# A pause on GpSimd and two later negations on ScalarE, ahead of the first out-projection of a fused attention and feed-forward kernel

## The chip, the cores and the metric

The kernel runs on one core of a Trainium2 chip. Time is device time in microseconds of one execution. The kernel before took 953.59 us, the median of three runs (953.5 to 954.16). The engines are named as in the profile: PE is TensorE (PEld its weight loads), DVE is VectorE, ACT is ScalarE, POOL is GpSimd, SP is SyncE, which here only issues transfers.

## The reference

Two blocks follow each other. The first is attention over 4 batches, 8 heads, 768 positions and 64 channels, in which a query sees only the keys that chose the same one of 16 centroids. The second is a feed-forward block over the resulting 3072 x 512 matrix.

```python
mask = q_assign[:, :, :, None] == k_assign[:, :, None, :]
scores = np.where(mask, scale * np.matmul(q, k.transpose(0, 1, 3, 2)), -1000000000.0)
attn = softmax(scores) ; x = (attn @ v) as (3072, 512)
h = x @ w_in                      # w_in 512 x 2048
sp = np.maximum(h, 0.0) + np.log1p(np.exp(-np.abs(h)))
g = h * erf(sp)                   # the gate
out = g @ w_out                   # w_out 2048 x 512
```

All of it is in float32.

## The kernel before

The attention ends about 404 us into the span. What follows is the feed-forward block, in six chunks of 512 tokens, n = 0 to 5. This case is about chunk 0 alone, from 404 to 500 us, and there about three stages: `hidden(0, 0)` and `hidden(0, 1)`, the in-projection of two lots of columns of `w_in`, and `project26(0)`, the out-projection.

**In-projection.** Each `hidden` runs four blocks (j = 0 to 3). A block is a product of 2 x 2 parts by seven matmul groups (Winograd's form of Strassen's scheme): `ORDER = (1, 2, 6, 7, 5, 3, 4)`. Each group of 4 matmuls writes one of eight PSUM banks, in turn ("bank" or "turned" in the profile), and DVE adds that bank into the result tiles `g` (the rows `g<-bank,g` and `g<-turned,g`), so that a bank is free again eight groups later. The first evacuation of a block is a plain copy, by ACT in `hidden(0, 0)` and by DVE in `hidden(0, 1)`.

**The side work.** After each of the 28 groups of a `hidden` one piece of the list `aside_work` is emitted, in order. These 28 places are called slots here, 0 to 27. Every engine runs its instructions in the order in which they are emitted. The gate of chunk 0 is made by quarters: first quarter (lot 0, blocks 0 and 1), second (lot 0, blocks 2 and 3), third (lot 1, blocks 0 and 1), fourth (lot 1, blocks 2 and 3). For each, ACT runs a Softplus and an Erf curve over two 128x1024 halves into `a_s` (for the fourth quarter into `x_own`), and DVE then makes four products `g<-a_s,g` of 128x512.

**The weight forms.** The out-projection multiplies `g` by sums and differences of quarter blocks of `w_out`, called forms. POOL makes them, two 128x512 operations a form:

- `early_forms26`, `next_forms26` (from 413 us) and then `all_sums`, four integer additions on `w_out`, which end at 430.85 us;
- `middle_forms26`: `of_last_rows` (5 operations: the rest of the forms y0 and y1, `ring[2]`, the rest of slot 0) and `of_all_rows` (4 operations: slot 7 and `ring[1]`);
- `late_forms26`: `streamed` (2 operations into `ring[2]`), `turned_over` (ACT: slot 4 becomes the negative of `ring[1]`, slot 5 that of a block of `w_out`) and `kept` (4 operations, slots 3 and 6, and then two accumulating transfers on POOL's queue: slot 4 += y0, slot 5 += y1; the rows `DMA_DIRECT2D more_out<-x_own`).

y0 and y1 lie in the second `x_own` tile; slots 0, 3 to 6 in `more_out`, `w_out` blocks and the like; the `ring` tiles are `g_more` in the profile.

**Out-projection.** `project26(0)` takes 26 steps, p = 0 to 25, of 8 matmuls each; the right factor of step p is `RIGHT[p]`: a slot, a block of `w_out`, or, from 100 up, a form held in a tile that is filled again during the stage by `rest_of_forms26`. That function also emits, behind certain steps:

- p = 2: SP fills y0 with a block of `w_out` (`x_own<-w_out`); ACT writes the negative of slot 0 into y1;
- p = 3: POOL issues y0 += slot 6 and y1 += slot 1 (`x_own<-more_out`); SP stores both to memory (`b_dram<-x_own`);
- p = 5: SP fills `ring[2]` (`g_more<-b_dram`); p = 7: SP fills `ring[1]` (`g_more<-w_out`), ACT writes the negative of slot 1 into the first `x_own`, and POOL issues `ring[1]` += that (`g_more<-x_own`).

Step p = 7 multiplies slot 4, p = 9 y0, p = 13 y1, p = 16 `ring[1]` as just filled, p = 19 slot 5. The left factors are `g` blocks, or sums of them that DVE makes (`left_step`; the first three of them run in slots 21 to 23 of `hidden(0, 1)`).

SP issues in this order: the five stores of forms, the fill of y0, the store of y0, the fills of `ring[2]` and `ring[1]`, the store of y1, and so on. The list below shows the functions at their lines; nearly all instructions bear line 123, that of the class `InOrder`, so they are told apart by tile and time.

Of the kernel before, what the change touches and what calls it, by code (L numbers as in the profile page):

```python
# [14 lines left out]
ALU = mybir.AluOpType  # L15
# [32 lines left out]
N_LATE = 4  # L48
# [83 lines left out]
def kernel(  # L132
# [13 lines left out]
    te, ve, ae, ge = (  # L146
        InOrder(tc, e, in_order) for e in (nc.tensor, nc.vector, nc.scalar, nc.gpsimd)
    )

    def pool(name, bufs, **kw):  # L150
        return ctx.enter_context(tc.tile_pool(name=name, bufs=bufs, **kw))
# [106 lines left out]
    for base, pattern, sign, op, fill in (  # L258
# [5 lines left out]
            out=first, in_=first, compare_op=op, fill=fill, base=base, pattern=pattern,  # L264
# [376 lines left out]
    def lefts(a11, a12, a21, a22, new):  # L641
        return {1: a11, 2: a12, 3: new[2], 4: a22, 5: new[0], 6: new[1], 7: a21}

    def rights(b11, b12, b21, b22, new):
        return {1: b11, 2: b21, 3: b22, 4: new[2], 5: new[0], 6: new[1], 7: b12}
# [4 lines left out]
    def w_in_parts(f, n):  # L650
        c1, c2 = slice(f * P, (f + n) * P), slice((HF + f) * P, (HF + f + n) * P)
        return (
            w_in[:, 0:HK, c1], w_in[:, HK:, c1], w_in[:, 0:HK, c2], w_in[:, HK:, c2],
            [more_in[:, i, :, c1] for i in range(3)],
        )

    def x_parts(n):
        x = x_of[n]
        return (
            x[:, 0:HK, 0:HT], x[:, 0:HK, HT:], x[:, HK:, 0:HT], x[:, HK:, HT:],  # L660
            [x_more[:, i] for i in range(3)],
        )

    g_of = {}

    ORDER = (1, 2, 6, 7, 5, 3, 4)
    aside_work = []
# [13 lines left out]
    def fresh(c11, c12, c21, c22, first=ae.copy):  # L681
        return {
            1: [lambda m: first(out=c12, in_=m)],
            2: [lambda m: plus_of(c11, m, c12)],
            6: [lambda m: onto(c12, m)],
            7: [lambda m: plus_of(c21, m, c12)],
            5: [lambda m: onto(c12, m), lambda m: plus_of(c22, m, c21)],
            3: [lambda m: onto(c12, m)],
            4: [lambda m: minus_of(c21, c21, m)],
        }  # L690

    def block(pieces, after, done=lambda i: None, pace=1):

        for i in ORDER:
            m = bank()
            pairs_of = pieces(i)
            for k, (lhsT, rhs) in enumerate(pairs_of):
                te.matmul(m, lhsT=lhsT, rhs=rhs, start=(k == 0), stop=(k == len(pairs_of) - 1))
            for f in after[i]:
                f(m)  # L700
            done(i)
            for work in aside_work[:pace]:
                work()
            del aside_work[:pace]

    def finish_aside():
        for work in aside_work:
            work()
        aside_work.clear()

    def hidden(n, lot, between={}, pace=1, **kw):

        for s in range(2):
            g_of[n, s, lot] = gp.tile([P, 2, FG, HT], F32, name="g")
        x = rights(*x_parts(n))
        for j in range(FG):
            w = lefts(*w_in_parts(lot * FG + j, 1))
            a, b = (g_of[n, s, lot] for s in range(2))
            block(
                lambda i: [(w[i][:, k], x[i][:, k]) for k in range(HK)],  # L720
                fresh(a[:, 0, j], b[:, 0, j], a[:, 1, j], b[:, 1, j], **kw), pace=pace,
            )
            between.get(j, lambda: None)()
# [4 lines left out]
    def idle(n):  # L728
        return [lambda: None] * n
# [12 lines left out]
    def slot(i):  # L742
        if i in BLOCK_OF:
            return w_block(BLOCK_OF[i])
        return more_out[:, HOME[i] // 2, (HOME[i] % 2) * FG : (HOME[i] % 2 + 1) * FG]
# [17 lines left out]
    def store_form(k, t):  # L763
        nc.sync.dma_start(out=stored_form(k), in_=t)

    def formed(o, a, b, sign, f):
        (plus_of if sign > 0 else minus_of)(o[:, f : f + 2], a[:, f : f + 2], b[:, f : f + 2], ge)

    def formed_whole(o, a, b, sign):
        for f in (0, 2):  # L770
            formed(o, a, b, sign, f)

    def onto_by_dma(o, a):
        ge.dma_start(out=o, in_=a, accum_op=ALU.add)

    def negated(o, a):
        ae.activation(out=o, in_=a, func=ACT.Copy, scale=-1.0)
# [4 lines left out]
    def form_places(n):  # L782
        t = x_of[n].rearrange("p k t -> p (k t)")
        return [t[:, i * FG * HM : (i + 1) * FG * HM].rearrange("p (f m) -> p f m", f=FG) for i in range(2)]
# [6 lines left out]
    def next_forms26():  # L791
        w, y = w_block, form_places(1)
        store_form(3, ring[0])
        formed_whole(slot(2), w(5), slot(1), 1)
        formed(y[0], w(3), w(7), -1, 0)
        formed(y[1], w(6), w(7), -1, 0)
        formed(slot(0), w(1), w(7), 1, 0)

    def middle_forms26():
        w, y = w_block, form_places(1)  # L800

        def of_last_rows():
            formed(y[0], w(3), w(7), -1, 2)
            store_form(7, y[0])
            formed(y[1], w(6), w(7), -1, 2)
            store_form(8, y[1])
            formed_whole(ring[2], w(6), y[0], 1)
            store_form(6, ring[2])
            formed(slot(0), w(1), w(7), 1, 2)

        def of_all_rows():
            formed_whole(slot(7), w(2), ring[2], -1)
            formed_whole(ring[1], w(0), w(4), 1)
            store_form(1, ring[1])

        return [of_last_rows, of_all_rows]

    def late_forms26():
        w, y = w_block, form_places(1)

        def streamed():
            formed_whole(ring[2], w(3), slot(2), -1)
            store_form(0, ring[2])

        def kept():
            formed_whole(slot(3), w(5), y[0], -1)
            formed_whole(slot(6), w(5), ring[1], -1)
            onto_by_dma(slot(4), y[0])
            onto_by_dma(slot(5), y[1])

        def turned_over():
            negated(slot(4), ring[1])
            negated(slot(5), w(1))

        return [streamed, turned_over, kept]
# [72 lines left out]
    def split_gate(lot, half):  # L908
        products_of = []

        def curves():
            soft, erf, products = gate26(0, lot, half)
            run(f() for f in soft + erf)
            products_of.extend(products)

        return curves, [lambda i=i: products_of[i]() for i in range(4)]

    def gate_work(n, lot, half, also=(), wait=0):
        soft, erf, products_of = gate26(n, lot, half)
        return [lambda: run([f() for f in soft + erf]), *idle(wait), *also, *idle(8 - len(also) - wait), *products_of]  # L920
# [392 lines left out]
    def run(work):  # L1313
        for _ in work:
            pass
# [136 lines left out]
    for e in range(2):  # L1452
        ve.tensor_copy(
            out=ccT[e * D : (e + 1) * D, :, e * C : (e + 1) * C],
# [8 lines left out]
    for r in (0, D):  # L1463
        for half in range(2):
            for e in range(2):
                c = r + half * Q + e * C
                ve.tensor_copy(
                    out=pick[r : r + D, half, e * D : (e + 1) * D].rearrange("p (n c) -> p n c", n=2)[:, :, 1 : C + 1],
# [44 lines left out]
    last = divide(u - 1)  # L1513
# [9 lines left out]
    behind = pool("behind", 1).tile([P, 1], F32, name="behind")  # L1523

    def finish_attention():
        run(last)
        banks[:] = [None] * 6 + turned
# [12 lines left out]
    def weights(n):  # L1540
        return [functools.partial(w, N_EARLY + n) for w in (size_and_rest, bounded, sign, shifted)]

    def all_sums():
# [4 lines left out]
    first_half, first_products = split_gate(0, 0)  # L1548
    second_half, second_products = split_gate(0, 1)
    aside_work += (  # L1550
        idle(3) + sum((weights(n) for n in range(N_LATE)), []) + [first_half, all_sums, *middle_forms26(), *idle(3), *first_products]
    )
    hidden(0, 0, {0: lambda: (finish_attention(), next_forms26())})

    def last_half():
        finish_aside()
        first_steps = [functools.partial(left_step, 0, x) for x, step in enumerate(LEFT_STEPS) if step[0] < 0]
        aside_work.extend(gate_work(0, 1, 0, first_steps, 6))

    aside_work += [second_half, *late_forms26(), *idle(4), *second_products]  # L1560
    hidden(0, 1, {1: last_half}, first=ve.tensor_copy)
    finish_aside()
    project26(0)
# [43 lines left out]
```

## Time and profile before

| | before |
|---|---|
| median of three runs | 953.59 us |
| the profiled execution | 953.27 us |
| its span | 951.6 us |
| PE busy | 942.7 us (99%) |
| DVE busy | 789.8 us (83%) |
| ACT busy | 556.4 us (58%) |
| POOL busy | 504.3 us (53%) |

The span runs from the first to the last instruction that the profile shows; the profiled execution's own time is 1.67 us longer. In a timeline each row gives the start and the duration in microseconds, the engine, the line, the operation, output and inputs, their shape, and how many equal instructions in a row were merged ("x2"); brackets behind it give the idle time of the engine before it and what ended that. "SPq" is a transfer as SP issues it; the duration is that of the issue, not of the transfer.

### The profile page before, as it was taken

Reading aid. Unit: us, or ns where it says so; the run is one execution under the profiler, and the core shown is the slowest. Engines: PE = TensorE matmul, PEld = TensorE weight load, DVE = VectorE, ACT = ScalarE, POOL = GpSimd, SP = SyncE. Lnnn points to the kernel's source line nnn. Section 1 sums busy time; section 2 is a strip of 40 time slices with the busy share of each in tenths; the row PEclk is TensorE's granted clock in tenths of the full one; section 3 lists DMA queues with packets and bytes.
Section 4 is the critical chain, followed back from the end, with each engine's and each line's share of the span. In section 5 each row is a group of like instructions: output and inputs, shape, how many; then the busy total and the mean of one; then the engine's idle time right before and its main releaser. Section 6 shows DMA issues by size and latency. Waiting matters only on the chain.

```text
span 951.6 us, 22455 instructions
## 1 busy us (share of the span) xinstructions
PE 942.7 (99%) x8938; PEld 719.8 (76%) x8938; DVE 789.8 (83%) x1402; ACT 556.4 (58%) x854; POOL 504.3 (53%) x355
## 2 busy tenths in 40 slices
PE   8999999999999999999999999999999999999998
PEld 3555555555555555588888888998999899989987
DVE  8888888888888887888886688688868977897887
ACT  3777777887777777566513642654257236525541
POOL 1688888888888888899109211360064016103600
PEclk9999999999999999999999999999999999999999
DMA  9355555555454522032786247353444436343533
GB/s 214 73 113 113 113 112 104 120 112 104 103 117 84 132 59 58 18 120 111 199 250 237 101 103 201 127 191 111 155 146 154 133 111 211 111 155 123 155 112 111
DMA packets 175385, 123.14 MB, mean 129 GB/s; under 512 B 131632, under 2 KB 142384, under 8 KB 175280
## 3 DMA queue, kind: packets, MB, share of 16 engines
q1 hardware_dynamic: 170912, 116.29, 43.4%
q0 software_dynamic: 1872, 4.98, 2.9%
q8 instruction: 71, 1.16, 0.5%
q10 hardware_dynamic: 2496, 0.43, 0.2%
q14 instruction: 34, 0.28, 0.1%
HBM read 91.78 MB, written 23.33 MB: 121 GB/s over the span
## 4 chain that ended last, share of the span: by engine, by line
PE 93%; DVE 2%; ACT 1%; issue 1%; DMA 1%; POOL 1%; SPq 0%; DVEq 0%; ACTq 0%; POOLq 0%
PE bank L123 40%; PE turned L123 31%; PE sc L123 17%; PE wide L123 6%; DVE g L123 1%; POOL more_out L123 1%; ACT a_s L123 0%; DMA g_more<-in_moe_w_out_dram 0%; DVE nmx L123 0%; DMA in_k<-in_k_dram 0%; ACT L123 0%; SPq L123 0%; DVE kT L123 0%; ACT osb L123 0%; ACT w_out L123 0%
## 5 line engine op out<-in xcount | busy, mean ns | idle before, releaser
L123 POOL TENSOR_TENSOR more_out<-more_out,pr 128x768 f32<-128x768 f32 x128 | 217.2, 1697 | 15.9 <-ACT pr L123 6.5
L123 DVE TENSOR_REDUCE nmx<-wide 128x2 f32<-128x1024 f32 (+2 forms) x189 | 179.4, 949 | 40.3 <-PE wide L123 39.3
L123 ACT ACTIVATE pr<-sc 128x768 f32<-128x768 f32 x192 | 148.7, 810 | 79.9 <-PE wide L123 66.0
L123 PE MATMUL turned<-pr,in_v 128*32 128x193 f32 x3072 | 144.8, 330 | 0.0
L123 POOL TENSOR_TENSOR g<-g 128x512 f32<-128x512 f32 x36 | 47.2, 1311 | 180.7 <-DVE g L123 178.8
L123 PEld LDWEIGHTS turned<-pr,in_v 128*32 128x32 f32 x3072 | 91.5, 109 | 51.0 <-issue 21.9
L123 DVE TENSOR_TENSOR g<-g 128x512 f32<-128x512 f32 x132 | 90.7, 687 | 22.5 <-PE bank L123 11.4
L123 PE MATMUL sc<-qT,kT 64*128 64x384 f32 x528 | 98.3, 485 | 0.0
L123 DVE TENSOR_TENSOR g<-bank,g 128x256 f32<-128x256 f32 (+1 forms) x128 | 64.6, 530 | 16.1 <-PE bank L123 9.5
L123 PE MATMUL bank<-g_more,g 128*128 128x256 f32 x320 | 75.6, 379 | 0.0
L123 PE MATMUL bank<-x_own,w_in 128*128 128x128 f32 (+1 forms) x440 | 74.0, 310 | 0.0
L123 ACT ACTIVATE a_s<-g 128x1024 f32<-128x1024 f32 x38 | 39.5, 1054 | 56.9 <-POOL g L123 45.3
L123 POOL TENSOR_TENSOR more_out<-pr,pr 128x768 f32<-128x768 f32 x32 | 58.9, 1842 | 20.2 <-ACT pr L123 20.2
L123 DVE TENSOR_TENSOR g<-a_s,g 128x512 f32<-128x512 f32 x76 | 67.3, 904 | 0.4 <-ACT a_s L123 0.4
L123 PEld LDWEIGHTS bank<-g_more,g 128*128 128x128 f32 x320 | 60.8, 190 | 8.3
L123 PEld LDWEIGHTS bank<-x_own,w_in 128*128 128x128 f32 x440 | 63.1, 191 | 4.6 <-issue 0.6
L123 PE MATMUL wide<-kv,qv 64*128 64x512 bf16 (+2 forms) x378 | 64.9, 327 | 1.0 <-ACT km L123 0.6
L123 PE MATMUL bank<-w_out,g 128*128 128x256 f32 x280 | 64.5, 379 | 0.0
L123 PE MATMUL wide<-km,qm 32*128 32x512 bf16 (+2 forms) x378 | 62.4, 326 | 0.0
L123 ACT ACT_TABLE_LOAD x40 | 51.3, 1283 | 18.3 <-DVE g L123 17.7
L123 PEld LDWEIGHTS sc<-qT,kT 64*128 64x128 f32 x528 | 47.8, 187 | 18.6 <-issue 0.9
L123 PEld LDWEIGHTS <-qv 64*128 64x128 bf16 x384 | 24.6, 93 | 47.1 <-issue 29.6
(239 smaller groups left out, 2030.4 us busy)
## 6 DMA issues: line engine op xcount, KB each, us to landing
g_more<-b_dram SPq DMA_DIRECT2D x52, 512.0 KB, 3.3
g_more<-w_dram SPq DMA_DIRECT2D x84, 256.0 KB, 2.9
x_own<-in_moe_w_in_dram SPq DMA_DIRECT2D x13, 512.0 KB, 5.4
in_v<-in_v_dram SPq DMA_DIRECT2D x32, 192.0 KB, 3.2
x_dram<-more_out SPq DMA_DIRECT2D x128, 48.0 KB, 1.7
x_own<-x_dram SPq DMA_DIRECT2D x6, 1024.0 KB, 5.8
in_k<-in_k_dram SPq DMA_DIRECT2D x59, 96.0 KB, 2.8
in_q<-in_q_dram SPq DMA_DIRECT2D x58, 96.0 KB, 5.0
```

What stands on the lines that cost most here:

```text
L123: ins = getattr(self.engine, name)(*args, **kw)
```

## The change

Four things change, all in the side work of chunk 0.

- POOL's `middle_forms26` leave slots 21 and 22 of `hidden(0, 0)`. They now stand in slots 6 and 7 of `hidden(0, 1)`, behind a new POOL instruction, `hold`, which adds one element per partition of the last product of the first quarter to itself, into the one-column tile `behind`, and so waits for that product.
- The four products of the first quarter, of which DVE had two in slots 26 and 27 of `hidden(0, 0)` and two in slots 0 and 1 of `hidden(0, 1)`, all stand in slots 0 to 3 of `hidden(0, 1)`.
- The second quarter's curves move from slot 2 to slot 4; `streamed` moves from slot 3 to slot 8; the second quarter's products stay in slots 10 to 13.
- `turned_over` and `kept` move from slots 4 and 5 to slots 15 and 16, behind the third quarter's curves in slot 14. ACT's two negations thus follow the third quarter's curves instead of preceding them.

The order of the instructions on PE and SP is the same as before. On POOL only `hold` is new.

```diff
@@ -1548,16 +1548,24 @@
     aside_work += (
-        idle(3) + sum((weights(n) for n in range(N_LATE)), []) + [first_half, all_sums, *middle_forms26(), *idle(3), *first_products]
+        idle(3) + sum((weights(n) for n in range(N_LATE)), []) + [first_half, all_sums, *idle(7)]
     )
     hidden(0, 0, {0: lambda: (finish_attention(), next_forms26())})
+
+    streamed, turned_over, kept = late_forms26()
 
     def last_half():
         finish_aside()
         first_steps = [functools.partial(left_step, 0, x) for x, step in enumerate(LEFT_STEPS) if step[0] < 0]
-        aside_work.extend(gate_work(0, 1, 0, first_steps, 6))
-
-    aside_work += [second_half, *late_forms26(), *idle(4), *second_products]
+        work = gate_work(0, 1, 0, first_steps, 6)
+        work[1:3] = turned_over, kept
+        aside_work.extend(work)
+
+    def hold():
+        last = g_of[0, 1, 0][:, 1, 0, 0:1]
+        ge.tensor_tensor(out=behind, in0=last, in1=last, op=ALU.add)
+
+    aside_work += [*first_products, second_half, hold, *middle_forms26(), streamed, *idle(1), *second_products]
     hidden(0, 1, {1: last_half}, first=ve.tensor_copy)
     finish_aside()
     project26(0)
```

## The prediction

> **What bounds the kernel now.** I read the page's span and chain first, then PE's waits over the whole span, then the timelines of PE, DVE, POOL, ACT and SP between 400 and 500 us, then SP's waits there. The first line is of the page, the second of its chain, the third of PE's waits.
>
> ```profile
> span 951.6 us, 22455 instructions
> PE 93%; DVE 2%; ACT 1%; issue 1%; DMA 1%; POOL 1%; SPq 0%; DVEq 0%; ACTq 0%; POOLq 0%
> PE turned L123 <- DVE g L123: 0.9, 2, 0.5
> ```
>
> PE carries the end. Whatever stops PE between here and the end is added to the time, and nothing behind gives it back. In the stages of the change PE waits only twice, 0.9 us together, both for DVE. That is all that the change can win there. PE's timeline shows the second of these waits, and then four steps of the first out-projection:
>
> ```profile
> 439.28 1.13 PE L123 MATMUL turned<-x_own,w_in 128*128 128x256 f32 x4 [0.55 <-DVE g L123]
> 454.98 1.89 PE L123 MATMUL bank<-more_out,g_more 128*128 128x256 f32 x8
> 467.07 1.89 PE L123 MATMUL bank<-more_out,g 128*128 128x256 f32 x8
> 470.52 1.89 PE L123 MATMUL bank<-x_own,g 128*128 128x256 f32 x8
> 482.61 1.89 PE L123 MATMUL bank<-g_more,g 128*128 128x256 f32 x8
> ```
>
> These are p = 0, p = 7 (slot 4), p = 9 (y0) and p = 16 (`ring[1]`, filled anew). From p = 9 to p = 16 there are seven steps in 12.09 us, 1.727 us each.
>
> **The gain.** DVE's timeline around the first quarter's products, around the second's, and later, where POOL has finished its additions:
>
> ```profile
> 430.04 0.42 DVE L123 TENSOR_TENSOR g<-turned,g 128x256 f32<-128x256 f32 x1 [3.42 <-ACT g L123]
> 432.63 1.23 DVE L123 TENSOR_TENSOR g<-a_s,g 128x512 f32<-128x512 f32 x1
> 434.12 1.42 DVE L123 TENSOR_TENSOR g<-a_s,g 128x512 f32<-128x512 f32 x1
> 435.46 0.41 DVE L123 COPY g<-bank 128x256 f32<-128x256 f32 x1
> 437.13 0.41 DVE L123 TENSOR_TENSOR g<-turned,g 128x256 f32<-128x256 f32 x1
> 443.11 1.17 DVE L123 TENSOR_TENSOR g<-a_s,g 128x512 f32<-128x512 f32 x1
> 449.23 0.41 DVE L123 COPY g<-bank 128x256 f32<-128x256 f32 x1
> 453.00 0.68 DVE L123 TENSOR_TENSOR g_more<-g 128x512 f32<-128x512 f32 x1
> 455.80 0.68 DVE L123 TENSOR_TENSOR g<-a_s,g 128x512 f32<-128x512 f32 x1
> ```
>
> A product takes 1.42 us beside POOL and 0.68 without it. A product with one evacuation comes every 437.13 - 435.46 = 1.67 us beside POOL; three such pairs without POOL lie between 453.00 and 455.80, 0.93 us each. DVE stands late at 430.04 because it waited for ACT. In the changed order the block's last evacuation comes at 432.63, where the first product stood; it and the next block's copy take 0.67 us, so the first product starts at 433.3, the fourth at 433.3 + 3 x 0.93 = 436.1, ending at 436.8. The bank that PE waited for at 437.60 is then evacuated at about 434.3. Both waits of PE go: -0.9 us.
>
> **POOL's delay.** POOL's timeline: the first and the last of its 15 additions after the pause, two in the middle, its transfers, and the same small instruction as `hold` from later in the kernel.
>
> ```profile
> 430.81 2.51 POOL L123 TENSOR_TENSOR x_own<-w_out 128x512 f32<-128x512 f32 x2
> 443.69 3.40 POOL L123 TENSOR_TENSOR g_more<-w_out,more_out 128x512 f32<-128x512 f32 x2
> 450.42 2.50 POOL L123 TENSOR_TENSOR more_out<-w_out,g_more 128x512 f32<-128x512 f32 x2
> 452.87 1.86 POOL L123 DMA_DIRECT2D more_out<-x_own  x2
> 462.19 0.84 POOL L123 DMA_DIRECT2D x_own<-more_out  x1 [7.46 <-DMA x_own<-w_out]
> 465.60 0.86 POOL L123 DMA_DIRECT2D x_own<-more_out  x1 [2.57 <-ACT g_more L123]
> 475.81 0.84 POOL L123 DMA_DIRECT2D g_more<-x_own  x1 [9.35 <-DMA g_more<-w_out]
> 500.25 0.19 POOL L123 TENSOR_TENSOR behind<-x_more 128x1 f32<-128x1 f32 x1 [9.33 <-DMA out_dram<-osb]
> ```
>
> `hold` itself costs 0.19 us, but behind it in POOL's queue stand all 15 additions and the five transfers. They begin at 436.8 + 0.2 = 437.05 instead of 430.81, 6.2 us later. An addition takes 1.25 us alone (2.51/2) and 1.70 us beside DVE's products (3.40/2). Which it is depends on where DVE's products now fall. ACT's timeline:
>
> ```profile
> 435.61 1.28 ACT L123 ACT_TABLE_LOAD   x1 [5.61 <-DVE g L123]
> 436.91 1.06 ACT L123 ACTIVATE a_s<-g 128x1024 f32<-128x1024 f32 x1
> 441.35 2.01 ACT L123 ACTIVATE a_s<-a_s 128x1024 f32<-128x1024 f32 x2
> 464.27 1.04 ACT L123 ACTIVATE x_own<-more_out 128x1024 f32<-128x1024 f32 x1
> ```
>
> The second quarter's table load waits for the first quarter's second product, which now ends at 434.9; two tables of 1.28 and three curves of 1.05 later, at 440.7, its first product can start (443.11 before). The four take 449.23 - 443.11 = 6.1 us with their evacuations before; I take 6.4, to 447.2. Up to the `left_step` at 453.00 DVE then needs 453.00 - 449.23 = 3.8 us, so that one comes at 451.0. POOL's count:
>
> - 437.05 to 440.7, alone: 2.9 additions.
> - 440.7 to 447.2, beside products: 6.5/1.70 = 3.8.
> - 447.2 to 451.0, alone: 3.0.
> - From 451.0 the remaining 5.2 stand beside the three `left_step`s and the third quarter's products, which before ran when POOL had finished: 5.2 x 1.70 = 8.8, to 459.85.
>
> The first accumulating transfer starts at 459.85 instead of 452.87: **7.0 us later**. If all 15 ran alone: 437.05 + 18.8, or 2.9 us later; all contended: 437.05 + 25.5, or 9.7 us later. I take the count between, nearer the contended row since DVE is busy throughout.
>
> [...]
>
> **What waits for POOL.** SP's timeline and SP's waits in this stretch, and the transfer list's row for the first two accumulations (median to landing):
>
> ```profile
> 457.60 0.70 SPq L780 DMA_DIRECT2D x_own<-w_out  x1
> 466.73 0.33 SPq L764 DMA_DIRECT2D b_dram<-x_own  x1
> 468.29 1.12 SPq L780 DMA_DIRECT2D g_more<-w_out  x1
> 470.46 0.33 SPq L764 DMA_DIRECT2D b_dram<-x_own  x1
> 480.31 0.32 SPq L764 DMA_DIRECT2D b_dram<-g_more  x1
> SPq L780 <- DMA more_out<-x_own: 10.0, 1, 10.0
> SPq L764 <- DMA x_own<-more_out: 9.3, 2, 8.3
> SPq L764 <- DMA g_more<-x_own: 7.7, 1, 7.7
> more_out<-x_own POOLq DMA_DIRECT2D x2, 512.0 KB, 5.7
> ```
>
> This is one chain with no slack inside: accumulate into slot 4 from y0 (452.87), landed and y0 filled anew (457.60), slot 6 accumulated onto it (462.19), landed (466.73); y0 is then stored, and behind that store in SP's queue `ring[1]` is filled (468.29), POOL accumulates onto it (475.81), landed (480.31). All its transfers are kept, each starts when the one before has landed, and PE is not in it, so a PE that is earlier does not help it. Its distances from PE's use are what can hide the 7.0 us:
>
> - slot 4: landed 457.60, used at 467.07: 9.5 us, enough.
> - y0: landed 466.73, used at 470.52: 3.8 us. p = 9 moves by 7.0 - 3.8 = +3.2 us.
> - `ring[1]`: landed 480.31, used at 482.61: 2.3 us. p = 16 moves by 7.0 - 2.3 = +4.7 us.
>
> The shifts do not add; the larger counts, and the 0.9 us gained is swallowed, as PE waits that much longer. One relief: the two first accumulations start 0.9 us apart (half of 1.86) and land after 4.7 and 6.7 us (median 5.7), so the second is in the way for 6.7 + 0.9 - 4.7 = 2.9 us after the first. y1's accumulation, now at 465.60 because of the negation at 464.27, will likewise come directly behind y0's, and be in the way of `ring[1]`'s fill for 2.9 us instead of 3.7 (466.73 to its store at 470.46). I take 0.8 us off: **+3.9 us**.
>
> **The negations on ACT.** They come behind the third quarter's curves, which run in about 447 to 453 now; they finish near 455 and POOL needs them only at 459.85. So they cost nothing; without that cover each would be 1.04 us. What is late is another negation, that at 464.27: it overwrites y1 and must wait until slot 5's accumulation has landed, 459.85 + 0.95 + 6.7 = 467.5. ACT's copies behind it, and DVE's rows that wait for them, come some 2.5 to 3 us later:
>
> ```profile
> 466.56 0.28 DVE L123 COPY osb<-g_more 128x256 f32<-128x256 f32 x1
> 468.96 2.86 DVE L123 TENSOR_TENSOR g<-g 128x512 f32<-128x512 f32 x4
> ```
>
> The first of these four makes p = 9's left factor, 469.6 before and 472 to 472.6 after. p = 9 waits for y0 till 473.7 anyway, so this is hidden; alone it would cost PE up to 2 us. The `left_step` that p = 0 needs is made at about 454.2, PE would be there at 454.98 - 0.9 = 454.1: 0.1 us, swallowed by p = 9.
>
> **The sum.** -0.9 (swallowed) + 7.0 - 2.3 - 0.8 = +3.9 us. The profiled execution (span 951.6, its own time 953.27) would go to 957.2; it lies 0.3 us under the median 953.59, which goes to **957.5**.
>
> **Rivals.**
>
> - *The delay is hidden, and the time is the same or a little better.* POOL catches up because most additions run alone: the transfer starts 2.9 us later, 2.9 - 2.3 - 0.8 is below nothing, and PE keeps up to 0.9 us: 952.7 to 953.7. For it: DVE finishes early in the new order. Against: the third quarter's products and `left_step`s lie where POOL now works. It decides where the first accumulation starts before 452.87 + 3.1 + 1.9 = 457.9.
> [...]
> - *The pause does not free DVE.* If the products' 1.42 us were not POOL's doing, they would stay at 1.67 us a pair, `hold` would end 3.0 us later, PE would keep its waits: 7.0 + 3.0 - 3.1 = +6.9, 960.5. Against: 0.68 us from 453.00 on, as soon as POOL's additions stop.
>
> **How the numbers follow.** My forecast 0.78, within 956.0 to 959.2; the hidden delay 0.13; the whole lock 0.06; the pause without effect 0.03. The bounds of the additions give -0.2 and 9.7 - 3.1 = +6.6, so 953.4 to 960.2. The range 953.9 to 959.9 leaves out about 2 in 10. A difference of 0.2% (1.9 us) is about what a measurement of this kernel can tell from none. Faster by that needs more than PE's 0.9 us of waiting, so 0.03; the same, the hidden case and the forecast's lowest end, 0.14; slower 0.83.
>
> **What would show it.** Right: PE without a wait near 437 to 440; DVE's first four products at 0.68 us; POOL idle for some 6 us before `hold`; the first accumulation near 460; PE waiting for the transfers into y0 at p = 9 (about 4 us from the earlier start) and for `ring[1]` at p = 16 (0.6 to 1.5 us). Wrong: no PE wait in the out-projection, or the accumulation before 457.9.

## The result, and the profile after

The changed kernel takes 959.99 us, the median of four runs (959.84 to 960.31), against 953.55 us for the kernel before in the same session (953.46 to 954.16). The ratio is 1.0067, with a 95% interval of 1.0055 to 1.008: slower by 6.4 us, where 3.9 were forecast. The range ended at 959.9.

The page's span and its chain, and below them PE's waits between 400 and 510 us (what was waited for: us in total, times, the longest), all of the kernel after:

```profile
span 958.1 us, 22457 instructions
...
PE 96%; DVE 2%; issue 1%; ACT 1%; DMA 0%; SPq 0%; DVEq 0%
```

```profile
PE bank L123 <- DVE osb L123: 4.3, 1, 4.3
PE bank L123 <- PE bank L123: 0.7, 1, 0.7
```

The two waits for DVE near 437 to 440 us are gone. In their place stand 0.7 us at p = 0 and 4.3 us at p = 9. PE's timeline after, at p = 0, 9, 10, 11 and 16, and then p = 11 of the kernel before:

```profile
454.01 1.97 PE L123 MATMUL bank<-more_out,g_more 128*128 128x256 f32 x8 [0.67 <-PE bank L123]
...
474.11 3.75 PE L123 MATMUL bank<-x_own,g 128*128 128x256 f32 x8 [4.32 <-DVE osb L123]
477.65 2.90 PE L123 MATMUL bank<-more_out,g 128*128 128x256 f32 x8
480.39 1.89 PE L123 MATMUL bank<-g_more,g 128*128 128x256 f32 x8
...
489.03 1.89 PE L123 MATMUL bank<-g_more,g 128*128 128x256 f32 x8
```

```profile
473.98 1.89 PE L123 MATMUL bank<-g_more,g 128*128 128x256 f32 x8
```

p = 9 starts 3.59 us later than before (474.11 - 470.52), p = 11 starts 6.41 us later, p = 16 6.42 us later. Nearly all of the loss is there by p = 11. It has two parts: the wait ahead of p = 9, and p = 9 and p = 10 themselves, which take 480.39 - 474.11 = 6.28 us instead of 2 x 1.727 = 3.45. That second part, 2.83 us, no term of the prediction held. The windows of the kernel after show it (length, busy time and count of PE, PEld, DVE, ACT and POOL, then the granted clock, the DMA share and GB/s):

```profile
472.00:473.00 1.00, 0.00 (x0) 0.00 (x0) 0.96 (x2) 0.00 (x0) 0.00 (x0) 0.93 1.08 197
473.00:474.00 1.00, 0.00 (x0) 0.00 (x0) 0.97 (x3) 0.77 (x2) 0.00 (x0) 0.50 1.03 197
...
479.00:480.00 1.00, 1.00 (x5) 0.84 (x4) 0.00 (x0) 0.00 (x0) 0.00 (x0) 0.65 0.95 362
480.00:481.00 1.00, 1.00 (x6) 0.90 (x5) 0.00 (x0) 0.36 (x1) 0.00 (x0) 1.00 1.10 402
```

The granted clock falls to 0.50 during PE's wait and is back at 1.00 only at 479.7, 5.6 us after p = 9 has begun. Half of 5.6 is the 2.8 us.

The wait itself comes from the chain of transfers that the prediction named. DVE, POOL and SP of the kernel after, in three timelines:

```profile
432.57 0.68 DVE L123 TENSOR_TENSOR g<-a_s,g 128x512 f32<-128x512 f32 x1
...
443.73 1.42 DVE L123 TENSOR_TENSOR g<-a_s,g 128x512 f32<-128x512 f32 x1
...
452.48 1.43 DVE L123 TENSOR_TENSOR g_more<-g,g_more 128x512 f32<-128x512 f32 x1
...
469.80 2.93 DVE L123 TENSOR_TENSOR g<-g 128x512 f32<-128x512 f32 x4
```

```profile
436.13 0.19 POOL L123 TENSOR_TENSOR behind<-g 128x1 f32<-128x1 f32 x1 [5.58 <-DVE g L123]
436.28 2.50 POOL L123 TENSOR_TENSOR x_own<-w_out 128x512 f32<-128x512 f32 x2
...
458.33 1.89 POOL L123 DMA_DIRECT2D more_out<-x_own  x2
469.45 1.73 POOL L123 DMA_DIRECT2D x_own<-more_out  x2 [9.22 <-DMA x_own<-w_out]
482.78 0.84 POOL L123 DMA_DIRECT2D g_more<-x_own  x1 [11.61 <-PE bank L123]
```

```profile
463.10 0.71 SPq L780 DMA_DIRECT2D x_own<-w_out  x1
474.04 0.33 SPq L764 DMA_DIRECT2D b_dram<-x_own  x1
475.68 1.10 SPq L780 DMA_DIRECT2D g_more<-w_out  x1
...
487.27 0.32 SPq L764 DMA_DIRECT2D b_dram<-g_more  x1
```

POOL pauses 5.6 us, the first quarter's products take 0.68 us, the accumulations start at 458.33 instead of 452.87 (+5.46), y0 is filled anew from 463.10, accumulated onto from 469.45, and stored at 474.04. PE starts p = 9 at 474.11, 0.07 us later. The row of the wait names a DVE copy, but the store of y0, which waits for the same transfer, shows what ended it. The fill of y0 to its accumulation took 469.45 - 463.10 = 6.35 us, where it took 462.19 - 457.60 = 4.59 before.

### The profile page after: what moved, and what is told of

The parts are those of the page before. It is cut to its first block, busy times and chain, and to the rows that moved or that the text cites. A ratio compares the mean times of both kernels' runs of the same rounds, so it can differ in the third digit from the quotient of the medians.

```text
span 958.1 us, 22457 instructions
## 1 busy us (share of the span) xinstructions
PE 945.2 (99%) x8938; PEld 722.0 (75%) x8938; DVE 792.1 (83%) x1402; ACT 555.8 (58%) x854; POOL 504.2 (53%) x356
## 4 chain that ended last, share of the span: by engine, by line
PE 96%; DVE 2%; issue 1%; ACT 1%; DMA 0%; SPq 0%; DVEq 0%
PE bank L123 42%; PE turned L123 31%; PE sc L123 17%; PE wide L123 6%; DVE g L123 1%; ACT x_own L123 0%; DVE nmx L123 0%; DMA in_k<-in_k_dram 0%; SPq L123 0%; DVE kT L123 0%; DVE g_more L123 0%; DVE osb L123 0%; DVE sims L123 0%; ACT km L123 0%; DVE hotT L123 0%
```

## The experiments

The medians of the kernel before in these sessions lie between 953.48 and 953.68 us. Unless the text says otherwise the edit is one to the kernel after.

**1. No pause.** `hold` is left out, all else stays.

```diff
-    aside_work += [*first_products, second_half, hold, *middle_forms26(), streamed, *idle(1), *second_products]
+    aside_work += [*first_products, second_half, *middle_forms26(), streamed, *idle(1), *second_products]
```

> The changed kernel without the pausing instruction, all else in its place. If the pause is the cause (POOL's accumulations start 5.5 us late, PE waits for y0 at p = 9, and its granted clock then halves), POOL starts near 431, the first accumulation waits only for ACT's negations and starts near 454, PE has no wait at p = 9, the granted clock stays 1.00 and the time is 953 to 954.7 us. If the later negations or the moved products are the cause, it stays above 957 us.

Measured: 958.57 us (958.07 to 958.62), ratio 1.0051 (1.0036 to 1.0066). A miss. One row of POOL's timeline and one of PE's say why:

```profile
457.75 1.89 POOL L123 DMA_DIRECT2D more_out<-x_own  x2 [4.68 <-ACT more_out L123]
```

```profile
473.85 3.54 PE L123 MATMUL bank<-x_own,g 128*128 128x256 f32 x8 [2.15 <-DVE osb L123]
```

POOL was done with its additions, and stood for 4.68 us until ACT's negations had come behind the third quarter's curves. So without the pause the rest of the change brings the accumulations nearly as late (457.75) as the pause does (458.33); in the kernel after, the pause covers it. Experiment 6 has the negations alone. PE's waits for DVE are back as well, 0.83 and 0.54 us near 447 and 450: it is the pause that freed DVE. And the clock fell to 0.50 here too, after a wait of only 2.15 us.

**2. A pause to the first product only.**

```diff
-        last = g_of[0, 1, 0][:, 1, 0, 0:1]
+        last = g_of[0, 0, 0][:, 0, 0, 0:1]
...
-    aside_work += [*first_products, second_half, hold, *middle_forms26(), streamed, *idle(1), *second_products]
+    aside_work += [first_products[0], lambda: (first_products[1](), hold()), *first_products[2:], second_half, idle(1)[0], *middle_forms26(), streamed, *idle(1), *second_products]
```

> The pause ends at the first of the four products instead of the fourth, nearly 3 us sooner. If the delay counts against a distance of about 3.8 us at p = 9, the first accumulation starts near 456, PE waits at most 2 us at p = 9, and the halved clock of 474 to 478 us stays away: 954 to 956 us. If each microsecond of delay costs a microsecond with no threshold, about 957 us; if the delay does not matter, 960 us as before.

Measured: 955.37 us (955.0 to 956.13), ratio 1.0018 (1.0009 to 1.0027).

```profile
455.90 1.91 POOL L123 DMA_DIRECT2D more_out<-x_own  x2
```

```profile
456.47 1.97 PE L123 MATMUL bank<-more_out,g_more 128*128 128x256 f32 x8 [1.34 <-issue]
```

The accumulations are 3.03 us late, y0 is stored at 470.63, 3.90 us late, and p = 9 does not wait. That is just past y0's slack of 3.8, but PE itself is late by then: p = 0 starts 1.49 us after its time in the kernel before, because the `left_step` takes 1.42 us beside POOL (at 454.95), where it took 0.68. Most of what is lost is lost there.

**3. The accumulations ahead of the last four additions.** In `kept`:

```diff
-            formed_whole(slot(3), w(5), y[0], -1)
-            formed_whole(slot(6), w(5), ring[1], -1)
             onto_by_dma(slot(4), y[0])
             onto_by_dma(slot(5), y[1])
+            formed_whole(slot(3), w(5), y[0], -1)
+            formed_whole(slot(6), w(5), ring[1], -1)
```

> The pause kept; POOL's two accumulating transfers are issued ahead of the four additions for slots 3 and 6 instead of behind them. If the chain through y0 is what the time hangs on, the first accumulation starts near 453 to 454, PE's waits near 437 to 440 stay away and none comes at p = 9: 952.4 to 953.6 us, at or under the kernel before. If DVE's left factors, ACT's copies or the forms of slots 3 and 6 are late as well, PE waits elsewhere and the time is above 954.5 us.

Measured: 956.22 us (955.28 to 956.83), ratio 1.0027 (1.0016 to 1.0037). Half a miss: the accumulations started at 453.66 and the clock stayed at 1.00 in the profiled execution (four of the eight had a mean of 0.998), but DVE, POOL and PE show a new loss (three timelines of this kernel).

```profile
455.83 5.24 DVE L123 TENSOR_TENSOR g<-a_s,g 128x512 f32<-128x512 f32 x1
```

```profile
455.16 2.92 POOL L123 TENSOR_TENSOR w_out<-w_out,x_own 128x512 f32<-128x512 f32 x2
457.62 2.90 POOL L123 TENSOR_TENSOR more_out<-w_out,g_more 128x512 f32<-128x512 f32 x2
```

```profile
464.35 1.97 PE L123 MATMUL turned<-w_out,g_more 128*128 128x256 f32 x8 [2.00 <-DVE g_more L123]
```

One product, 0.68 us long when alone, lasted 5.24 us beside the four additions and ended only after they had. PE paid for it 2.00 us at p = 5. At p = 9 it waited 1.01 us more, and not for y0, which was stored at 469.55, but for DVE's left factor, whose row starts at 471.94: the delay that the prediction had named as hidden.

**4. PE kept busy during the wait.** Ahead of p = 9 come 18, in a second kernel 9, more calls of a matmul into the bank that p = 9 then overwrites, so that nothing they compute is used.

```diff
+            for f in range(18 if n == 0 and p == 9 else 0):
+                te.matmul(m, lhsT=left26(n, 2)[:, f % FG], rhs=slot(2)[:, f % FG], start=True, stop=True)
             for f in range(FG):
                 te.matmul(m, lhsT=lhs[:, f], rhs=rhs[:, f], start=(f == 0), stop=(f == FG - 1))
```

> The changed kernel with 18 more matmuls on PE ahead of step p = 9, into the bank that p = 9 then starts anew, so that PE works through most of its 4.3 us wait. If the idle time is what halves the granted clock, p = 9 and p = 10 take 1.73 us each again instead of 3.54 and 2.74, PE then waits about 1 us for the refilled ring tile at p = 16, and the time is 957.5 to 959 us. If the slow steps come from the transfers that run at the same time, they stay slow and the time stays at 960 us.

Measured: 960.67 us (960.42 to 961.41), ratio 1.0076 (1.0062 to 1.009). The filling was too long for the wait, so the time tells nothing, but PE's rows do:

```profile
470.07 7.93 PE L123 MATMUL bank<-more_out,g 128*128 128x256 f32 x36
477.84 1.89 PE L123 MATMUL bank<-x_own,g 128*128 128x256 f32 x8
```

The transfers of this stretch run as before, and p = 9 and p = 10 take 1.73 us each. So it was not the transfers that slowed the two steps. With 9 calls instead:

> As the run with 18 more matmul calls ahead of p = 9, which lasted 7.8 us and so overfilled the wait; now 9 calls, 3.9 us, a little less than the 4.3 us wait. If idleness halves the granted clock, p = 9 starts when y0 lands (about 474), p = 9 and p = 10 take 1.73 us each, PE waits 0.8 to 1.2 us for the refilled ring tile at p = 16, and the time is 957.8 to 958.8 us. If the loss belongs to the start of the step and not to idleness, it stays at 960 us.

Measured: 958.66 us (958.12 to 960.13), ratio 1.0058 (1.0041 to 1.0074).

```profile
469.68 4.05 PE L123 MATMUL bank<-more_out,g 128*128 128x256 f32 x18
474.20 1.97 PE L123 MATMUL bank<-x_own,g 128*128 128x256 f32 x8 [0.47 <-DVE osb L123]
476.00 1.89 PE L123 MATMUL bank<-more_out,g 128*128 128x256 f32 x8
...
487.13 1.97 PE L123 MATMUL bank<-g_more,g 128*128 128x256 f32 x8 [0.60 <-DVE g L123]
```

p = 9 starts where it did (474.20), and p = 9 and p = 10 go at full speed. Now the wait at p = 16 appears that the prediction had: in the kernel after, PE was so late from the slow steps that it found `ring[1]` already filled. p = 16 starts 489.03 - 487.13 = 1.90 us earlier, and the medians differ by 1.3 us, though one execution with the 9 calls took 960.13 us at a clock of 1.00, so the intervals overlap. The lost clock costs 2.8 us where it falls; 1.9 of these are left at p = 16, by these two traces, and 1.3 in the medians.

**5. The delay alone.** The kernel before, with slot 6's form made three times over, which is four additions more, so that POOL's accumulations come late and the order of all else stays.

```diff
             formed_whole(slot(6), w(5), ring[1], -1)
+            for _ in range(2):
+                formed_whole(slot(6), w(5), ring[1], -1)
             onto_by_dma(slot(4), y[0])
```

> The kernel before, with slot 6's form made three times instead of once ahead of the accumulations: four more additions on POOL, 5 to 6.8 us, no pause and nothing else moved. [...] If DVE's or ACT's new order is needed for the loss, the time stays under 955.5 us.

Measured: 958.05 us (957.53 to 959.09), ratio 1.0049 (1.0034 to 1.0064).

```profile
473.99 1.97 PE L123 MATMUL bank<-x_own,g 128*128 128x256 f32 x8 [1.40 <-DVE g L123]
...
487.03 1.97 PE L123 MATMUL bank<-g_more,g 128*128 128x256 f32 x8 [0.71 <-DMA g_more<-x_own]
```

The accumulations came at 459.45, 6.58 us late. By the prediction's arithmetic p = 16 then moves by 6.58 - 2.3 = 4.3; it moved by 487.03 - 482.61 = 4.42, and the median by 4.57. The two shifts do not add here, as said: the clock stayed at 1.00. The wait at p = 9 was 1.40 us and not 4.32 as in the kernel after, because PE had already waited 1.33 us at p = 0 for a `left_step` beside the added additions. So POOL's lateness alone costs 4.6 us, without the new order on DVE and ACT; a clock of 0.50 came behind the longer waits, 4.32 us in the kernel after and 2.15 in experiment 1.

**6. The negations alone.** The kernel before, with `turned_over` and `kept` behind the third quarter's curves.

```diff
-        aside_work.extend(gate_work(0, 1, 0, first_steps, 6))
+        work = gate_work(0, 1, 0, first_steps, 6)
+        work[1:3] = turned_over, kept
+        aside_work.extend(work)
...
-    aside_work += [second_half, *late_forms26(), *idle(4), *second_products]
+    streamed, turned_over, kept = late_forms26()
+    aside_work += [second_half, streamed, *idle(6), *second_products]
```

> The kernel before with one part of the change alone: ACT's two negations, and POOL's additions for slots 3 and 6 and its accumulations, are emitted behind the third quarter's curves; no pause, products where they were. If the late negations alone hold POOL back, as the run without the pause suggests, the first accumulation starts when the first negation ends, near 456 to 457.8, 3 to 5 us late, PE waits 1 to 3 us at p = 9, and the time is 955.5 to 959 us. If the negations matter only together with the moved products, the accumulation stays near 453 to 454.5 and the time is 953.3 to 954.3 us.

Measured: 956.3 us (955.45 to 956.77), ratio 1.0029 (1.0018 to 1.0039).

```profile
456.04 1.89 POOL L123 DMA_DIRECT2D more_out<-x_own  x2 [3.00 <-ACT more_out L123]
```

POOL waits 3.00 us for ACT. The accumulations are 3.17 us late, but y0 is stored at 471.82, 5.09 us late, since its fill is slow here too (see the end), and PE waits 1.08 us at p = 9 and 0.93 at p = 16. Without the pause the later negations cost 2.8 us by themselves.

**7. The pause alone.** The negations return to their place ahead of the third quarter's curves.

```diff
-        work[1:3] = turned_over, kept
...
-    aside_work += [*first_products, second_half, hold, *middle_forms26(), streamed, *idle(1), *second_products]
+    aside_work += [*first_products, second_half, hold, *middle_forms26(), streamed, turned_over, *second_products[:3], lambda: (second_products[3](), kept())]
```

> The changed kernel with ACT's negations back ahead of the third quarter's curves (slot 9), the pause kept. If the pause alone delays the additions, the first accumulation still starts near 458, PE waits about 4 us at p = 9 and the clock halves: 959.5 to 961.5 us, since ACT now also waits for the ring form before the third quarter's curves. If the late negations are what delays POOL, it starts near 454 and the time is under 956 us.

Measured: 958.24 us (957.4 to 958.84), ratio 1.0049 (1.0034 to 1.0064), less than expected. POOL's row and PE's p = 9 and p = 10:

```profile
458.50 1.89 POOL L123 DMA_DIRECT2D more_out<-x_own  x2
```

```profile
473.09 1.96 PE L123 MATMUL bank<-x_own,g 128*128 128x256 f32 x8 [2.12 <-DVE g L123]
474.89 1.89 PE L123 MATMUL bank<-more_out,g 128*128 128x256 f32 x8
```

The accumulations are as late as in the kernel after, but y0 arrives about a microsecond earlier, and after 2.12 us of waiting the clock is still 1.00. The profiled execution, 957.40 us, is the lowest of the four; two of the others had a mean clock of 0.998 and took 957.73 and 958.75 us.

**8 to 10. Spreading DVE's products without a pause.** These look for what the change could have kept: its 0.9 us. In 8 the kernel before only has the first quarter's products moved to slots 0 to 3 of `hidden(0, 1)`, and the work behind them follows two slots later. In 9 (shown against 8) the second quarter's are spread too, over slots 10, 12, 14 and 15, and in 10 (against 9) the `left_step`s besides come earlier, in slots 19 to 21.

```diff
-        idle(3) + sum((weights(n) for n in range(N_LATE)), []) + [first_half, all_sums, *middle_forms26(), *idle(3), *first_products]
+        idle(3) + sum((weights(n) for n in range(N_LATE)), []) + [first_half, all_sums, *middle_forms26(), *idle(5)]
...
-    aside_work += [second_half, *late_forms26(), *idle(4), *second_products]
+    aside_work += [*first_products, second_half, *late_forms26(), *idle(2), *second_products]
```

> The kernel before with the moved products alone: the first quarter's four products one to a slot in slots 0 to 3 of the second lot, the second quarter's curves behind them, no pause, negations and accumulations where they were. If the order of DVE's products alone removes PE's two waits near 437 to 440, they are gone; but with the products still at 1.4 us beside POOL, DVE is late again near 448 to 450, so 0.3 to 0.9 us of waits come there: 952.9 to 953.7 us, the same as before. The first accumulation stays near 453. If the moved products were a cause of the loss, over 954.5 us.

```diff
-        aside_work.extend(gate_work(0, 1, 0, first_steps, 6))
+        curves, *later = gate_work(0, 1, 0, first_steps, 6)
+        aside_work.extend([*second_products[2:], curves, *later[2:]])
...
-    aside_work += [*first_products, second_half, *late_forms26(), *idle(2), *second_products]
+    aside_work += [*first_products, second_half, *late_forms26(), *idle(2), second_products[0], *idle(1), second_products[1]]
```

> As the moved products alone, and the second quarter's four products spread as well (slots 10, 12, 14 and 15), with the third quarter's curves two slots later. If the waits near 448 to 450 come from four products in a row, they go too, no wait is left between 430 and 500 us and the time is 952.4 to 953.1 us, 0.5 to 0.9 us under the kernel before. If the later third curves hold up DVE or the out-projection's left factors, PE waits at p = 0 or p = 9 and it is 953.6 us or more.

```diff
-        aside_work.extend([*second_products[2:], curves, *later[2:]])
+        aside_work.extend([*second_products[2:], curves, *idle(2), *first_steps, *idle(2), *later[9:]])
```

> As the version with both quarters' products spread, and the three sums that DVE makes for the out-projection's first left factors emitted two slots sooner (slots 19 to 21). There PE waited 0.8 us at p = 0 for the second of them. If that was the last place where DVE's lateness shows, PE has no wait over 0.2 us between 430 and 500 us and the time is 952.4 to 953.1 us, under the kernel before. If the lateness only moves on, as it moved from 437 to 448 and from there to 455, PE waits 0.5 to 0.9 us at one of the steps p = 1 to p = 9 and the time is 953.2 to 953.7 us.

Measured: 953.51 us (953.24 to 954.1), ratio 1.0 (0.9991 to 1.0009); 953.41 us (952.95 to 954.12), 0.9996 (0.9987 to 1.0005); 954.0 us (953.08 to 954.7), 1.0004 (0.9995 to 1.0013). None can be told from the kernel before. PE's waits in the three, one fence each:

```profile
447.97 1.13 PE L123 MATMUL bank<-x_own,w_in 128*128 128x256 f32 x4 [0.38 <-DVE g L123]
449.64 1.13 PE L123 MATMUL bank<-x_own,w_in 128*128 128x256 f32 x4 [0.54 <-DVE g L123]
```

```profile
454.90 1.97 PE L123 MATMUL bank<-more_out,g_more 128*128 128x256 f32 x8 [0.83 <-PE bank L123]
```

```profile
483.13 1.97 PE L123 MATMUL bank<-g_more,g 128*128 128x256 f32 x8 [0.91 <-ACT g_more L123]
```

In 8 the 0.37 + 0.55 us of the kernel before become 0.38 + 0.54 ten microseconds later, where DVE's products still run beside POOL's additions. In 9, which was hoped to have no wait left, there are 0.83 us at p = 0, behind a `left_step` that takes 1.52 us beside POOL. In 10 only 0.35 of these are left, and p = 0 starts at 454.18, 0.80 us sooner than in the kernel before. The 0.91 us at p = 16 are no lateness of DVE. SP's timeline of 10 shows that the store of y1 now stands ahead of the fill of `ring[1]`:

```profile
470.83 0.32 SPq L764 DMA_DIRECT2D b_dram<-x_own  x1
471.32 0.60 SPq L780 DMA_DIRECT2D g_more<-w_out  x1
```

The fill starts at 471.32 instead of 468.29, and `ring[1]` is stored at 483.01 instead of 480.31. So 10 had won most of a microsecond up to p = 9 and lost it to another order of two transfers; its median lies above both ranges that were expected. No version beat the kernel before, and 10 with SP's old order was not tried.

## Why the prediction failed, step by step

- *The gain.* Right in kind: both waits are gone, the products take 0.68 us, and it is swallowed. But it was more than 0.9 us. PE's timeline of the kernel before, around the two waits:

```profile
435.34 1.89 PE L123 MATMUL bank<-x_own,w_in 128*128 128x256 f32 x8
437.60 1.13 PE L123 MATMUL turned<-x_more,more_in 128*128 128x256 f32 x4 [0.37 <-DVE g L123]
...
440.25 1.03 PE L123 MATMUL bank<-x_more,more_in 128*128 128x256 f32 x4
```

The four groups from 435.34 to 440.25 take 4.91 us; groups that wait for nothing follow each other every 0.86 us (the next starts at 441.11), so four take 3.45. The two waits cost 1.46 us, and the idle time in brackets does not show all of it.

- *POOL's delay, 7.0 us.* Right in kind, too large: `hold` came at 436.13 and not 436.8, and 15 additions took 458.33 - 436.28 = 22.05 us, not 22.8. It is 5.46 us, inside the bounds of 2.9 to 9.7.
- *The chain has no slack inside, and y0 has 3.8 us.* The slack held; the chain's own length did not. y0 landed at 474.04, 7.31 us late, because its fill took 1.76 us longer than before (more on that at the end). The two errors nearly cancel: p = 9 moved by 3.59 us where 3.2 were said.
- *"The shifts do not add; the larger counts."* **This is the step that failed.** It took p = 9 to p = 16 at seven times 1.727 us, whatever PE had waited before, although it expected a wait of about 4 us there: it has no term for the clock. After 4.3 us without work PE ran p = 9 and most of p = 10 at a clock of 0.50, and the 2.83 us do add to p = 9's shift: 3.59 + 2.83 = 6.42, more than p = 16's. Experiments 4 and 5 show it from both sides: with PE kept busy, or with y0 as late and a shorter wait, the two steps run at full speed and the larger shift counts.
- *`ring[1]`, +4.7, less 0.8 of relief.* `ring[1]` landed 487.27 - 480.31 = 6.96 us late, and 6.96 - 2.3 = 4.7; the wait of 0.60 us in the second kernel of experiment 4 shows it. The relief was smaller: from y0's store to `ring[1]`'s accumulation 482.78 - 474.04 = 8.74 us against 9.08, so 0.34 us. With 7.31 - 0.34 - 2.3 = +4.7 the forecast without the clock would have been 958.3, and that kernel took 958.66.
- *The negations "cost nothing".* Right only as long as the pause is there. The cover was named, but its price was given as 1.04 us each; without it the price is the wait for the third quarter's curves, 3.00 to 4.68 us of POOL's time, and 2.8 us of the whole.
- *p = 0, 0.1 us.* It was 0.67. The `left_step` at 452.48 ended at 453.91, near the 454.2 said; but PE was done with the in-projection at 454.01 - 0.67 = 453.34 and not at 454.1, in part because its gain was larger than said.
- *The left factor of p = 9 at 472 or later.* It was ready sooner: the first of the four at 469.80 ends near 470.5. It was hidden, as said.
- *The rivals.* The accumulations came at 458.33, past the 457.9 from which the hidden delay would have needed them earlier. The pause did free DVE (0.68 us a product). No run shows the whole lock, to which the prediction gives 0.06: in the kernel after a product and an addition that met mostly took 1.42 and 1.70 us, as before.

## What to carry to other kernels

Before delaying an engine that issues transfers, follow each of them to the step that uses its data, and compare the delay with that distance; against a distance of 3.8 us at p = 9, a delay of POOL of 5.5 us cost 4.3 us of waiting. The distance alone does not settle it: with delays of 3.0 and 3.2 us the tile came 3.9 and 5.1 us late, as transfers between took longer (experiments 2 and 6). If what is left over is a wait of TensorE of some 2 us or more (behind 2.15 and 4.32 us the clock was at 0.50 in experiment 1 and in the kernel after, behind 2.00 and 2.12 it was at 1.00 in the traces of 3 and 7), add a term for the halved clock behind it, and ask whether a later wait hides part of that. Waits of half a microsecond (0.37 and 0.55 us) that come from two engines that slow each other down (a product of 0.68 us took 1.42, an addition of 1.25 us 1.70) mostly moved on when the work was moved about: they came back ten microseconds later (8) and at p = 0 (9). Where they did go (10), a change in the order of transfers took the gain; check that order again after every edit.

## What the hardware showed beyond that

**The length of the wait did not alone decide whether the clock fell.** The trace's record of the granted clock, in microseconds of the span, and PE's idle time laid against it (worked out from PE's rows at these places; the span's last 4 us, when PE has ended, are left out). The last column lays stretches of 3.413 us end to end from the first rise on, and has the one with the most idle time:

```
kernel            first at 1.00   then at 0.50       lasts   PE idle          idle in one stretch of 3.413
after             5.24            472.87 to 479.69   6.827   469.79-474.11    3.08 (469.45-472.87)
1, no pause       6.45            474.07 to 477.49   3.413   471.70-473.85    2.15 (470.66-474.07)
7, pause alone    8.18            not                -       470.97-473.09    1.43 (468.98-472.40)
3, accumulate     5.12            not                -       462.35-464.35    1.85 (462.50-465.92)
```

In both kernels that lose the clock it stays at 1.00 for 467.626 us, which is 137 times 3.4133, and is then lost for one or two times 3.413; in the kernel after it then stays at 1.00 for 477.866 us, 140 times, and in the kernel before for 945.492 us from the first rise, 277 times. Cut into such stretches, the two kernels that lost it had 2.15 and 3.08 us of idleness in one of them, and the two that kept it had 1.43 and 1.85. Experiments 1 and 7 wait 2.15 and 2.12 us, and differ in where a stretch ends. That the idleness in such a stretch decides is the author's estimate from these four traces; no run varied the gap by itself. This also fits that the mean clock differs between executions of one kernel: 1.0 in one of the four of experiment 1 (958.07 us) and 0.997 in three (958.55 to 958.62 us). By the estimate the limit lies between 1.85 and 2.15 us in a stretch, and as a gap of 4.32 us has at least 2.16 us in one of two stretches, the kernel after loses the clock wherever they begin; its four executions had 0.996 to 0.997. Cut the same way, the other nine traces have at most 1.39 us in a stretch, and keep the clock. The limit may be lower than 2.15: the four executions of experiment 3 with 0.998 lost about what one stretch at 0.50 costs (0.5 x 3.413 / 954.6 = 0.0018), and the one trace of it has a wait of 2.00 us; theirs were not kept. In the kernel after, the stretch from 472.87 on held 1.24 us of waiting, less than the 1.43 and 1.85 with which the clock stayed at 1.00, and the clock returned only after the next one, in which PE did not wait. In experiment 1 it returned after one stretch.

**One product was held through four additions.** In experiment 3 a DVE product lasted 5.24 us, from 455.83 to 461.07, while POOL went from one addition to the next (455.16 to 460.52); in the kernel after the six products beside additions took 1.09 to 1.83 us. What makes the difference was not tried.

**The fill of y0 took 5.8 us instead of 4.1** in the kernel after, 5.8 to 6.1 in experiments 1, 4 and 6, and 4.3 to 4.6 in 2, 3, 5 and 7. The transfer list has its row in the kernel after and before, one fence each, and in the windows of the kernel after next to nothing moves in the last 1.4 us. The last fence is again of the transfer list of the kernel after, 450 to 492 us (packets, MB, share):

```profile
x_own<-w_out SPq DMA_DIRECT2D x1, 512.0 KB, 5.8
```

```profile
x_own<-w_out SPq DMA_DIRECT2D x1, 512.0 KB, 4.1
```

```profile
468.00:469.40 1.40, 1.40 (x8) 1.23 (x7) 1.37 (x5) 0.60 (x2) 0.00 (x0) 1.00 0.02 6
```

```profile
q8 instruction: 1, 0.02, 0.1%
```

The trace's single packets have a candidate. The fill goes in 16 shares, each closed by a packet of 4 bytes; outside experiment 3, where another transfer mixes in, 15 of them are closed within 3.8 us of the issue in every kernel. The last one is closed after 5.3 to 5.6 us in the kernel after and in experiments 1, 4 and 6, and after 3.7 to 4.1 us in the others. In just the slow ones a packet of 16 KB on the queue `q8 instruction`, 0.9 to 1.0 us long, starts 2.5 to 2.8 us after the issue, in the midst of the fill (465.55 in the kernel after); in the others it starts 3.9 to 4.9 us after it, when the fill is through. So it probably holds up one share. That was not tested, nor what decides when it comes; the slow fill is 1.76 us of the 7.31 by which y0 was late.
